# A gated linear attention with a cosine layer: transposes through DRAM, a shorter pipeline, group 0 in chunks, a later weight guard

## The chip, the cores and the metric

The kernel runs on one core of one Trainium2 chip. The time is the device time of one execution in microseconds, as the median of several runs. The names used below are TensorE or PE (matmuls), PEld (weight loads), DVE (VectorE), ACT (ScalarE), POOL (GpSimd) and SP (the engine that issues nearly all transfers, in order).

## The reference

```python
scale = np.minimum(mag, 0.999) / (mag + 1e-06)          # mag = |a|
for t in range(S):                                      # B, H, S, D = 4, 8, 768, 48
    S_re, S_im = a * S (complex) + k[t] v[t]^T
    y[t] = q[t] @ S_re
x = y as (3072, 384)
h = x @ w_in                                            # w_in (384, 2048), double precision
out = (h * cos(h)) @ w_out                              # w_out (2048, 384), double precision
```

The kernel works in chunks of 128 steps, two chunks to a group, twelve groups. For each group it makes *gates* (log, sums by matmul, exponentials, angles, sine and cosine), *squares* (k and q times the gates, transposed to kT and qT), *chunks* (scores, state, output yT), x (yT put into the layout of the layer, xT), the *first layer* (`hp`, with the cosine gate) and the *second layer* (`op`). The weights come in double precision and are converted to single precision by bit operations. A guard looks at their exponents.

## The kernel before

The squares are transposed in 32 x 32 blocks by DVE, and 12 transfers of 32 KB per chunk and tensor put the blocks in place, from SBUF to SBUF:

```python
def f_transpose(n, name):
    tr = ft.tile([C, NR, H, 32], F32, tag="tr", name="tr")
    nc.vector.transpose(out=tr, in_=...)
    ...
    for a in range(Q4):
        for b in range(NR):
            nc.sync.dma_start(out=place[ts(b, 32), a], in_=tr[ts(a, 32), b])
```

x goes the same way, in ten transfers. The order of work is four stages deep; one iteration works on four groups:

```python
for it in range(NG + 3):
    g, c, m, o = it, it - 1, it - 2, it - 3
    ...                                   # g_log, g_prod, g_angle of group g
    for i in range(G): mm2(o, i)          # second layer of group o
    weave((gates(g), 0.0, 0.5), (chunks(c), 0.0, 1.0),
          (weights.get(it, ()), 0.0, 1.0),
          ([mm1(m, jp) for jp in range(NJ // 2)], 0.0, 1.0))   # first layer of group m
```

`weave` sorts the pieces of its parts by their place between the two numbers. The program that builds the kernel (the builder) takes this as a priority and may move a piece ahead. What it decides is then each engine's fixed order.

## Time and profile before

| | before |
|---|---|
| time | 821.7 us (821.4 to 823.4) |
| period of a group in the dense part | 56.9 us, of which PE busy 55.6 |
| first matmul of the second layer | 169 us |
| PE busy in all | 697 us of 823 |

### The profile page before, as it was taken

The page shows a single profiled execution, that of the slowest core. Times are in us where ns is not written, and L with a number is a line of the kernel's source. Part 1 is how long each engine was busy: PE and PEld are TensorE (multiplying, and loading weights), DVE is VectorE, ACT ScalarE, POOL GpSimd, SP SyncE. Part 2 cuts the span into 40 slices and gives each one's busy share as a digit, 9 for nine tenths or more (in the row PEclk, how much of TensorE's full clock was granted, in tenths as well). Part 3 has the DMA queues.
Part 4 walks back from the last instruction along what each step waited for, and adds up shares of the span by engine and source line. Part 5 has one row for each costly group of instructions (what it writes and reads, how often), then busy time and mean ns, then how long its engine had stood idle before and what let it go on. Part 6 is the DMA issues. An engine that isn't in the chain of part 4 may idle for free.

```text
span 823.1 us, 10293 instructions
## 1 busy us (share of the span) xinstructions
PE 697.1 (85%) x3464; PEld 514.9 (63%) x3464; DVE 488.7 (59%) x754; ACT 376.4 (46%) x576; POOL 146.6 (18%) x96
## 2 busy tenths in 40 slices
PE   1217286766899999999999989999999999999997
PEld 0006174534575785876867857858758668677674
DVE  2876454957685574864954856757658458234060
ACT  5552615663666345453571562464545624123140
POOL 1341124322401113003012021040040120000000
PEclk9956576897999999999999999999999999999999
DMA  9624257545632722623625427226236231210000
GB/s 178 128 47 71 45 128 192 129 103 115 164 80 49 150 45 62 119 49 68 112 51 92 84 49 135 42 54 123 49 62 110 51 73 30 49 40 21 20 0 23
DMA packets 251481, 65.67 MB, mean 80 GB/s; under 512 B 230414, under 2 KB 247823, under 8 KB 251419
## 3 DMA queue, kind: packets, MB, share of 16 engines
q1 hardware_dynamic: 250818, 64.62, 38.6%
q8 instruction: 29, 0.48, 0.3%
q10 hardware_dynamic: 600, 0.30, 0.2%
q14 instruction: 34, 0.27, 0.1%
HBM read 36.51 MB, written 4.76 MB: 50 GB/s over the span
## 4 chain that ended last, share of the span: by engine, by line
PE 53%; SPq 15%; DVE 12%; ACT 9%; issue 4%; DMA 3%; POOL 3%; DVEq 0%; ACTq 0%; POOLq 0%
PE hp L823 20%; PE op L841 18%; SPq L753 12%; PE sc L764 3%; ACT rs L629 2%; PE lgs L672 2%; POOL m L656 2%; PE phs L709 2%; PE yp L778 2%; PE sp L795 2%; DVE gate L833 2%; PE phs L712 1%; PE yp L782 1%; ACT L628 1%; SPq L545 1%
## 5 line engine op out<-in xcount | busy, mean ns | idle before, releaser
L823 PE MATMUL hp<-xT,w_in 128*128 128x256 f32 x1152 | 272.9, 390 | 16.0 <-DMA xT<-yT 8.6
L841 PE MATMUL op<-w_out,gate 128*128 128x384 f32 x768 | 256.3, 490 | 17.3 <-POOL w_out L600 17.1
L823 PEld LDWEIGHTS hp<-xT,w_in 128*128 128x128 f32 x1152 | 218.4, 194 | 53.1 <-DVE gate L835 8.7
L841 PEld LDWEIGHTS op<-w_out,gate 128*128 128x128 f32 x768 | 145.8, 191 | 118.5 <-POOL w_out L600 21.3
L829 ACT ACTIVATE turn<-hp,quarter_b 128x512 f32<-128x512 f32 x96 | 65.5, 683 | 91.4 <-PE hp L823 90.2
L629 ACT ACTIVATE gate<-gate 128x512 f32<-128x512 f32 x96 | 60.2, 628 | 102.4 <-DVE gate L833 102.3
L835 DVE TENSOR_TENSOR gate<-hp,gate 128x512 f32<-128x512 f32 x96 | 65.5, 685 | 38.8 <-ACT gate L629 38.4
L831 DVE TENSOR_SCALAR gate<-turn 128x512 f32<-128x512 f32 x96 | 40.7, 427 | 61.9 <-ACT turn L829 61.0
L672 PE MATMUL lgs<-m,sums 128*128 128x384 f32 x48 | 25.1, 657 | 52.2 <-POOL m L656 52.2
L833 DVE TENSOR_TENSOR gate<-turn,gate 128x512 f32<-128x512 f32 x96 | 67.2, 702 | 1.7
L801 POOL TENSOR_TENSOR state<-state,end 96x384 f32<-96x384 f32 x16 | 16.8, 1050 | 266.2 <-DVE state L799 175.2
L844 ACT ACTIVATE ot<-op 128x384 f32<-128x384 f32 x24 | 11.6, 484 | 114.4 <-PE op L841 114.4
L764 PEld LDWEIGHTS sc<-qT,kT 96*128 96x128 f32 x384 | 53.0, 206 | 15.6 <-issue 9.8
L764 PE MATMUL sc<-qT,kT 96*128 96x128 f32 x384 | 53.5, 290 | 7.4 <-issue 4.1
L656 POOL TENSOR_TENSOR m<-m,rs 128x768 f32<-128x768 f32 x12 | 21.7, 1808 | 178.0 <-ACT rs L629 178.0
L672 PEld LDWEIGHTS lgs<-m,sums 128*128 128x128 f32 x48 | 10.6, 245 | 64.7 <-POOL m L656 59.8
L714 DVE TENSOR_SCALAR ph<-phs 128x384 f32<-128x384 f32 x24 | 13.3, 555 | 55.7 <-PE phs L712 40.8
L709 PE MATMUL phs<-sq,sums 128*128 128x384 f32 x48 | 23.0, 570 | 27.2 <-DVE sq L700 27.2
L766 DVE TENSOR_TENSOR atm<-sc,causal 128x512 f32<-128x512 f32 x48 | 32.6, 682 | 18.8 <-PE sc L764 18.6
L659 DVE SCALAR_TENSOR_TENSOR sq<-mag,sq 128x768 f32<-128x768 f32 x12 | 11.5, 958 | 49.1 <-POOL mag L658 49.1
L778 PE MATMUL yp<-atm,v 128*48 128x128 f32 x384 | 38.2, 288 | 0.0
L729 POOL TENSOR_TENSOR Q<-k,Q 128x768 f32<-128x768 f32 x12 | 25.6, 2130 | 55.8 <-ACT rs L697 19.7
(75 smaller groups left out, 812.6 us busy)
## 6 DMA issues: line engine op xcount, KB each, us to landing
kT<-tr SPq DMA_DIRECT2D x288, 32.0 KB, 2.0
qT<-tr SPq DMA_DIRECT2D x288, 32.0 KB, 1.8
raw<-in_moe_w_in_dram SPq DMA_DIRECT2D x12, 512.0 KB, 4.8
raw<-in_moe_w_out_dram SPq DMA_DIRECT2D x16, 384.0 KB, 3.8
re<-in_a_re_dram SPq DMA_DIRECT2D x24, 192.0 KB, 3.0
im<-in_a_im_dram SPq DMA_DIRECT2D x24, 192.0 KB, 4.1
k<-in_k_dram SPq DMA_DIRECT2D x24, 192.0 KB, 4.0
q<-in_q_dram SPq DMA_DIRECT2D x24, 192.0 KB, 4.6
```

The costliest lines, as they stand in the source:

```text
L629: chain(nc.scalar.activation(func=func, **kw))
L672: nc.tensor.matmul(ps, lhsT=sums, rhs=x["lg"][:, ts(i, DM)], start=True, stop=True)
L709: nc.tensor.matmul(ps, lhsT=sums, rhs=x["turn"][:, ts(i, DM)], start=True, stop=first)
L753: nc.sync.dma_start(out=place[ts(b, 32), a], in_=tr[ts(a, 32), b])
L764: nc.tensor.matmul(ps[:, h], lhsT=y["kT"][:, hh * HH + h], rhs=queries(y, hh * HH + h), start=True, stop=True)
L778: nc.tensor.matmul(ps[ds(side * 64, D), p], lhsT=vals[:, 2 * p + side], rhs=y["atm"][:, 2 * p + side], start=True, stop=(state is None))
L823: nc.tensor.matmul(ps[:, ji], lhsT=w_in[:, dc, ts(jp * 2 + ji, C)], rhs=x["xT"][:, dc].rearrange("p g t -> p (g t)"), start=(dc == 0), sto ...
L829: nc.scalar.activation(out=turn, in_=ps, func=AF.Identity, scale=INV_TWO_PI / in_scale, bias=quarter_b)
L831: nc.vector.tensor_scalar(out=cs, in0=turn, scalar1=ROUND, scalar2=ROUND, op0=ALU.add, op1=ALU.subtract)
L833: nc.vector.tensor_tensor(out=cs, in0=turn, in1=cs, op=ALU.subtract)
L835: nc.vector.tensor_tensor(out=gate, in0=ps, in1=cs, op=ALU.mult)
L841: nc.tensor.matmul(ps, lhsT=X[g]["gate"][j // 2][:, j % 2, ts(i, C)], rhs=w_out[:, j], start=(j == 0), stop=(j == NJ - 1))
```

## The change

The intent: SP is relieved of its many small transfers; a group's chunks and its first layer lie in the same iteration, so that the pipeline is one stage shorter; group 0 goes through the gates chunk by chunk with its products on DVE; the guard leaves the start and reads the weights a second time later. The core of the diff (cut: the pass of `i, n` through all gate functions, the split of group 0, temporaries that share buffers):

```diff
-        for a in range(Q4):
-            for b in range(NR):
-                nc.sync.dma_start(out=place[ts(b, 32), a], in_=tr[ts(a, 32), b])
+        moved = rows_d.tile([Q4, D2, n * H, 32], F32, tag="moved", name="moved", bufs=3)
+        nc.sync.dma_start(out=moved.rearrange("q (r b) x j -> (q r) b x j", b=NB), in_=tr)
+        if name == "kT":
+            for q4 in range(Q4):
+                nc.sync.dma_start(out=X[g][name][:, ds(i * H, n * H), q4], in_=moved[q4])
+        else:
+            nc.sync.dma_start(out=X[g][name][:, :, ds(i * H, n * H)],
+                              in_=moved.rearrange("q c x j -> c q x j"))
 ...
     def f_xt(g):
-        (ten transfers yT -> xT)
+        moved = rows_d.tile([HH, 2, D, G * C], F32, tag="x", name="x")
+        for side in range(2):
+            nc.sync.dma_start(out=moved[:, side]..., in_=X[g]["yT"]...)
+        nc.sync.dma_start(out=xt..., in_=moved...)
 ...
-    weights = {1: parts[:-NJ], 2: parts[-NJ:]}
-    for it in range(NG + 3): ...
+    conversions = {(-1, 1): into, (0, 0): back[:NJ // 2], (0, 1): back[NJ // 2:]}
+    for c in range(-1, NG + 1):
+        ...
+        weave((gates_a(c + 1), 0.0, 0.3),
+              (chunks(c) if c >= 0 else (), 0.0, 0.9),
+              (extra(c, 0), 0.0, 1.0),
+              (second(c - 1), 0.0, 1.0))
+        weave((gates_b(c + 1), 0.0, 0.5),
+              (extra(c, 1), 0.0, 1.0),
+              (first(c) if c >= 0 else (), 0.0, 1.0))
```

An iteration now has two halves. The first holds the gates up to the phase sums of the next group, the chunks of this one and the second layer of the last one. The second half holds the rest of the gates and this group's first layer. `extra` is conversion of weights at first and guard later.

## The prediction

> **What bounds the kernel now.** I read the page's forty slices first, then busy time in three stretches, then the chain of work that ended last, and last the timeline of the sync engine (SP) in the first 80 us. Rows of the slices:
>
> ```profile
> PE   1217286766899999999999989999999999999997
> PEclk9956576897999999999999999999999999999999
> DMA  9624257545632722623625427226236231210000
> ```
>
> Each digit is 20.6 us. The matrix engine (PE) is a tenth or two busy in the first three slices, around 70% until the tenth, and at 90% or more in nearly every slice after that. So there are two regimes, and the border is near 258 us, where the gate sums of the fifth group start. Busy time on both sides of it (columns: stretch, its length, then busy time and instruction count of PE, weight loads, DVE, ACT, POOL, the granted clock, the DMA share, GB/s):
>
> ```profile
> 0.00:257.80 257.80, 149.24 (x678) 106.75 (x678) 164.25 (x263) 134.08 (x216) 70.56 (x54) 0.80 0.52 112
> 257.80:713.00 455.20, 444.54 (x2320) 332.92 (x2321) 292.77 (x438) 216.21 (x318) 74.87 (x42) 1.00 0.39 75
> 713.00:823.00 110.00, 103.32 (x467) 75.18 (x465) 31.64 (x53) 26.10 (x42) 1.21 (x1) 0.99 0.08 23
> ```
>
> The middle stretch is eight groups: 56.9 us each, of which PE works 444.54 / 8 = 55.6 us. It is bound by PE at 98%. Twelve groups of 55.6 us are 667 us of PE work at full clock. From 257.8 us on PE does 444.5 + 103.3 = 548 us of it, so before 257.8 us it did 119 us' worth, at a mean clock of 0.80. The start therefore loses 258 - 119 = 139 us; the rest loses 565 - 548 = 17 us, 6 of them in the check of the flags at the end. 667 + 139 + 17 = 823. Whatever the change gains has to come out of the 139.
>
> What fills the start: the chain of waits names SP's queue, and SP's timeline shows why.
>
> ```profile
> PE 53%; SPq 15%; DVE 12%; ACT 9%; issue 4%; DMA 3%; POOL 3%; DVEq 0%; ACTq 0%; POOLq 0%
> ```
>
> ```profile
> 41.84 7.98 SPq L753 DMA_DIRECT2D kT<-tr  x12
> 49.92 7.53 SPq L753 DMA_DIRECT2D qT<-tr  x12
> 57.55 7.85 SPq L753 DMA_DIRECT2D kT<-tr  x12
> 65.50 7.86 SPq L753 DMA_DIRECT2D qT<-tr  x12
> 73.40 3.03 SPq L685 DMA_DIRECT2D end<-row  x6
> ```
>
> Twelve transfers of 32 KB take 7.8 us to issue, 0.65 us each, back to back for 31.6 us. During this the DMA engines are only 23 to 32% busy (windows 40 to 80 us). Scores of chunk 0 wait for the 24th issue (PE starts them at 64.8), those of chunk 1 for the 48th (75), and the weights wait behind. Even in the steady part SP issues for 48 x 0.65 + 10 x 0.63 (x) + 6 x 0.48 (end) + some 8 (loads, out) = 48 of 57 us.
>
> ```profile
> kT<-tr SPq DMA_DIRECT2D x288, 32.0 KB, 2.0
> raw<-in_moe_w_in_dram SPq DMA_DIRECT2D x12, 512.0 KB, 4.8
> raw<-in_moe_w_out_dram SPq DMA_DIRECT2D x16, 384.0 KB, 3.8
> out_dram<-ot SPq DMA_DIRECT2D x24, 192.0 KB, 3.2
> xT<-yT SPq DMA_DIRECT2D x72, 48.0 KB, 2.0
> ```
>
> The last column is the time from issue to landing; it sizes the new transfers below.
>
> **What the Trainium skill says.** "Perfetto Trace Analysis", section What "DMA-bound" means, counts a solid issuing track as a bound of its own, apart from the movement of data; the trace agrees (SP solid for 31.6 us, engines a third busy). "DMA: Bandwidth & Descriptors", Rules for kernel authors, wants many small transfers joined, since under 64 KB one pays mostly overhead, and a transfer that reads what another wrote must wait for its semaphore. The first agrees: 32 KB cost 0.65 us of queue and 192 KB loads about the same. The second is the price of going through DRAM. "TensorE: Matmul & The Clock Gate", What's actually happening, has a half-rate state after idle windows; here the clock is 0.50 from 40 to 60 us and 1.00 when dense. "SBUF — State Buffer", section SBUF: two separate sides, says that DVE and GpSimd lock each other out; the same weight operation on DVE takes 0.42 us alone and 2.03 us beside GpSimd's product at 23.2 us.
>
> **The change part by part.**
> Squares: per group 48 issues become 2 writes, 4 reads of kT and 1 of qT; x 10 become 3; end 6 become 2. 64 issues become 12. At 0.5 to 1 us each SP saves about 40 - 9 = 31 us per group. In the steady part this is worth nothing directly, as PE is the bound there. In the start it is on the path.
> Bytes: each square now moves twice, in packets of 2 KB except kT's read, which still scatters 128 B. Per group DMA work falls out as: loads 10 x 1.05 us (192 KB at the 184 GB/s of the first 20 us at full share), kT read 6144 packets of 128 B at about 22 ns over 16 engines, 8.5 us (an estimate from what is left of 0.42 x 57 us of a steady group), other square traffic 2.4 MB at some 300 GB/s, 8 us. About 27 us per group in all.
> Group 0 per chunk: operations of 0.96 us become two of 0.55, products go from POOL (1.8 to 2.2 us) to DVE. First results come out some 4 us sooner. Scores of chunk 0: phase sums now at 30.6 us come near 22, stacked by 27, then write 3.5, kT read 3.5, qT write and read 6: near 42 instead of 64.8.
> Guard later: 28 DVE operations (17.4 us) and 28 ACT ones (18.4 us) leave the start; 12.6 MB are read again in groups 3 to 9, two tiles per half iteration, where DMA has room (0.4 busy).
> One stage fewer: the first layer matmul of group 0 follows its chunks in the same iteration. It starts at 128 us now. New: chunks end near 58 us, x is there near 68. Gates of 20.7 us of first-layer work end near 95 if DVE keeps up: DVE has in this iteration 20 (gates of group 1) + 15 (w_out, 16 x 0.94) + 4 (scores) + 14.6 (8 x 1.82) = 54 us after some 45 in the iteration before, so about 100. DMA until then: 2.5 groups of loads 26, weights 12.6 MB at 300 GB/s 42, two groups of squares 33, x 3: 104 us of 16 full engines. DMA and DVE both say PE gets dense at 105 to 115 us; I take 112, with 45 us' worth of PE work done (gates of two groups 9, chunks 10 to 15, first layer 21). Loss in the start 67 instead of 139: gain 72.
> The cost: before, x had a whole iteration to arrive. Now it lies between chunks and first layer of one group: copies to yT 1.2, one more issue 0.5, write as out<-ot 3.2, read as a 384 KB weight tile 3.8, semaphores 0.3: 9 us, each group. After the second chunk's output PE still has two pieces of the second layer (2 x 8 matmuls x 0.323 = 5.2 us) and often part of the 3.2 us of phase sums. Exposed: 1 to 4 us, plus delay by other traffic. I take 3 us x 11 = 33, which includes the 1.3 us of gaps that a group has now.
> Sum: 667 + 67 + 33 + 6 = 773.
>
> **Rivals.**
> (a) x hidden after all: the builder already moves work a long way (second-layer matmuls run ahead of gate sums emitted before them; the squares of the next group start 25 us early). If it fills the gap, 1.3 us per group: about 755.
> (b) x, or kT and qT, late: SP waits in order, so a wait for a DRAM write holds the read behind it; guard tiles of 512 KB sit in front of x. The square chain is now write, wait, read, write, wait, read, some 18 us where it used to be 31 of issue. At 7 us per group: 815, all the gain nearly gone. For it: a period of 57 has to hold gates, squares, chunks, x and first layer over two iterations, about 103 of 114 us by my count, which is little slack. Against: SP is freed by 31 us.
> (c) DMA bandwidth or DVE holds the start longer, PE dense only at 130: 790.
> (d) Second half of an iteration bound by DVE (14.6 + 8 = 22.6 us against 20.7 of PE): 2 us per group, 795 with the rest; unlikely to add fully, since the stack can be moved ahead.
>
> **Range and chances.** Most likely between the sum and a little of (b): 775. Eight in ten: 745 (a shorter start, x hidden) to 812 (b, or c and d together). Faster by over 2% means under 805: 0.84. Within 2%: 0.11. Slower: 0.05; that would need over 9 us lost in each group.
>
> **What would show it.** PE's slices at 90% from the sixth on; first hp matmul near 70 us and first op near 100; SP for the squares down from 576 issues to about 90; PE's total near 690. Idle of hp put down to DMA xT: 20 to 40 us shows the price of x; 70 or more shows (b), near 5 shows (a). PE idle put down to qT or kT would show the squares late. I am wrong if PE's dense part has a period over 61 us per group, or if it starts after 130.

## More of the kernel before

The prediction shows the slices, the windows and SP's queue. One more view: the order of PE inside one iteration of the dense part. These are lines of PE's timeline (start, length, engine and line, operation, names, shapes, count, and the idle time before it with what ended it):

```profile
314.67 1.56 PE L672 MATMUL lgs<-m,sums 128*128 128x384 f32 x4 [1.69 <-POOL m L656]
316.07 12.42 PE L841 MATMUL op<-w_out,gate 128*128 128x384 f32 x38
328.32 0.81 PE L709 MATMUL phs<-sq,sums 128*128 128x384 f32 x2
...
334.39 1.06 PE L764 MATMUL sc<-qT,kT 96*128 96x128 f32 x8
335.28 2.76 PE L823 MATMUL hp<-xT,w_in 128*128 128x256 f32 x12
337.87 1.48 PE L795 MATMUL sp<-v,ks 128*96 128x48 f32 x16
339.19 2.82 PE L823 MATMUL hp<-xT,w_in 128*128 128x256 f32 x12
```

Between the log sums (lgs) and the phase sums (phs), whose inputs ACT and DVE have to make, PE does 12.4 us of second layer. Between the steps of a chunk (sc, sp) it does first layer of another group. The only wait in the iteration is the 1.69 us at lgs. (In these views the trace has two records for each matmul of the code: 96 hp for the 48 of a group, 64 op for 32.)

## The result, and the profile after

The changed kernel takes 849.4 us (844.7 to 853.9, 4 runs) against 821.7. The ratio is 1.033, with a 95% interval of 1.027 to 1.039: it is slower, clear of noise. A ratio is the mean time of one kernel's runs over that of the other's of the same rounds, so it is not quite the ratio of the medians that are quoted. The profiled execution is the fastest of the four, with a span of 842.9 us. The four runs spread over 9 us and differ in their mean granted clock, the share of full speed that PE was given: 0.959 and 0.957 in the two faster ones, 0.940 and 0.932 in the two slower. So the profile shows somewhat less loss than the median has. Its slices:

```profile
PE   1236298799889989989989989989989989989996
PEclk9999599999989999999999999999989999999999
DMA  9877796896680680580670671670770670170100
```

Each digit is now 21.1 us. The start is better than before: PE is at 70% or more from the sixth slice on, where before it stood at 60 to 80% from the sixth to the eleventh. But from there on the row repeats "989", with a dip in every third slice, once in each group, and this goes on to the end. Before, the row was nines. The same in one stretch of both dense parts, first before, then after (columns as in the prediction):

```profile
386.90:699.50 312.60, 304.73 (x1625) 231.11 (x1625) 206.75 (x313) 151.55 (x222) 49.36 (x28) 0.99 0.39 74
```

```profile
386.90:699.50 312.60, 282.65 (x1421) 208.25 (x1420) 192.98 (x262) 143.18 (x204) 53.45 (x26) 0.97 0.48 102
```

PE was busy 97.5% of this stretch and is now busy 90%, and in the same 312.6 us it gets through 1421 matmuls instead of 1625. No other engine took its place: DVE is 62% busy, ACT 46%. Six periods, taken from one lgs to the sixth after it, are 63.1 us each (331.99 to 710.81), against 56.9 before (314.67 to 655.91). Eleven periods at 6.2 us more make 68 us. That is where the time went. What PE waits for in the dense part of the changed kernel, from 192 to 815 us (total us, times, longest):

```profile
PE hp L850 <- DMA xT<-x: 29.8, 10, 4.1
PE phs L727 <- DVE tan L719: 14.8, 9, 3.6
PE lgs L692 <- POOL lg L675: 11.7, 9, 1.3
```

And PE's order in one iteration, which answers to the one shown of before:

```profile
426.43 22.41 PE L850 MATMUL hp<-xT,w_in 128*128 128x256 f32 x96 [4.01 <-DMA xT<-x]
448.68 1.06 PE L790 MATMUL sc<-qT,kT 96*128 96x128 f32 x8
449.57 7.91 PE L870 MATMUL op<-w_out,gate 128*128 128x384 f32 x24
458.77 1.56 PE L692 MATMUL lgs<-lg,sums 128*128 128x384 f32 x4 [1.29 <-POOL lg L675]
460.17 1.06 PE L790 MATMUL sc<-qT,kT 96*128 96x128 f32 x8
461.06 6.62 PE L870 MATMUL op<-w_out,gate 128*128 128x384 f32 x20
469.07 0.91 PE L727 MATMUL phs<-tan,sums 128*128 128x384 f32 x2 [1.40 <-DVE tan L719]
...
480.80 5.43 PE L870 MATMUL op<-w_out,gate 128*128 128x384 f32 x16
488.61 1.35 PE L850 MATMUL hp<-xT,w_in 128*128 128x256 f32 x5 [2.38 <-DMA xT<-x]
```

All 96 matmuls of the first layer now stand in one block behind x. Ahead of them are the last 16 of the second layer, 5.4 us. PE stands still three times in a group: at lgs, at phs (20 matmuls lie between the two instead of 38) and at hp. There is a fourth loss that no wait shows. The 96 hp matmuls take 22.4 us here. They take 20.99 us in the groups where the pause before them left the clock alone (group at 741.72 below). In the eleven groups from 169 us on, the excess over 20.99 adds up to 15.7 us; in the six periods measured above it is 1.6 us a group. In one such block the granted clock is 0.50 from 300.4 to 302.4 us and 1.00 before the pause and from 303.4 on. The way of x in one group, from the chain of work that ended last (start, length, what):

```profile
734.46 0.59 ACT yT L812
735.06 3.04 DMA x<-yT
738.11 0.02 SPq L841
738.13 0.03 issue
738.16 3.52 DMA xT<-x
741.68 0.04 issue
741.72 20.99 PE hp L850 x96
```

Store 3.0, load 3.5, with the copies 7.9 us from the last output (733.8) to the first hp.

In the start x of group 0 has a trouble of its own. SP's timeline:

```profile
80.45 0.38 SPq L837 DMA_DIRECT2D x<-yT  x1
87.45 3.44 SPq L590 DMA_DIRECT2D raw<-in_moe_w_out_dram  x3
90.94 0.42 SPq L837 DMA_DIRECT2D x<-yT  x1
92.18 2.27 SPq L590 DMA_DIRECT2D raw<-in_moe_w_out_dram  x2
95.26 0.38 SPq L841 DMA_DIRECT2D xT<-x  x1
```

The outputs are complete at 77 us. The second store of x goes out 10.5 us after the first, because loads of w_out stand between the two and SP, taking its list in order, waits for their buffers. hp starts at 100 after 23.3 us of idle PE.

### The profile page after: what moved, and what is told of

The parts are those of the page before. It is cut to its first block, busy times and chain, and to the rows that moved or that the text cites. A ratio compares the mean times of both kernels' runs of the same rounds, so it can differ in the third digit from the quotient of the medians. Undisturbed runs are those within 1.5% of the kernel's fastest.

```text
span 842.9 us, 9481 instructions
## 1 busy us (share of the span) xinstructions
PE 700.1 (83%) x3464; PEld 514.9 (61%) x3464; DVE 528.2 (63%) x757; ACT 382.6 (45%) x589; POOL 154.7 (18%) x92
## 5 line engine op out<-in xcount | busy, mean ns | idle before, releaser
L850 PE MATMUL hp<-xT,w_in 128*128 128x256 f32 x1152 | 270.1, 399 | 56.2 <-DMA xT<-x 56.2
L850 PEld LDWEIGHTS hp<-xT,w_in 128*128 128x128 f32 x1152 | 230.7, 201 | 97.7 <-DMA xT<-x 63.2
L870 PEld LDWEIGHTS op<-w_out,gate 128*128 128x128 f32 x768 | 142.3, 190 | 91.9 <-issue 2.2
L675 POOL TENSOR_TENSOR lg<-lg,rs 128x768 f32<-128x768 f32 x11 | 20.0, 1814 | 374.8 <-ACT rs L637 374.2
L812 ACT COPY yT<-yp 48x512 f32<-48x512 f32 x48 | 27.7, 578 | 54.2 <-PE yp L808 41.0
L727 PE MATMUL phs<-tan,sums 128*128 128x384 f32 x48 | 24.8, 607 | 31.8 <-DVE tan L719 29.3
L768 DVE STREAM_TRANSPOSE tr<-qs 128x1536 f32<-128x1536 f32 (+1 forms) x13 | 26.7, 2052 | 36.3 <-DMA moved<-tr 36.3
L692 PE MATMUL lgs<-lg,sums 128*128 128x384 f32 x48 | 23.2, 609 | 28.0 <-POOL lg L675 15.7
L827 POOL TENSOR_TENSOR state<-state,end 96x384 f32<-96x384 f32 x16 | 26.6, 1663 | 103.3 <-DVE state L825 60.1
L792 DVE TENSOR_TENSOR atm<-sc,causal 128x512 f32<-128x512 f32 x48 | 32.8, 684 | 10.5 <-PE sc L790 10.5
L821 PEld LDWEIGHTS sp<-v,ks 128*96 128x96 f32 x320 | 31.9, 174 | 3.9 <-issue 2.4
L677 DVE SCALAR_TENSOR_TENSOR tan<-mag,tan 128x768 f32<-128x768 f32 (+1 forms) x13 | 11.6, 895 | 35.9 <-POOL mag L676 35.8
```

The lines of the kernel that those rows point to most:

```text
L792: nc.vector.tensor_tensor(out=y["atm"][:, ts(hh, HH)], in0=ps, in1=causal.unsqueeze(1).to_broadcast([C, HH, C]), op=ALU.mult)
L812: nc.scalar.copy(out=X[g]["yT"][half, :, i], in_=ps[half])
L821: nc.tensor.matmul(ps[:, h], lhsT=keys, rhs=X[g]["v"][:, i, h], start=True, stop=True)
L850: nc.tensor.matmul(ps[:, ji], lhsT=w_in[:, dc, ts(jp * 2 + ji, C)], rhs=x["xT"][:, dc].rearrange("p g t -> p (g t)"), start=(dc == 0), sto ...
L870: nc.tensor.matmul(ps, lhsT=X[g]["gate"][j // 2][:, j % 2, ts(i, C)], rhs=w_out[:, j], start=(j == 0), stop=(j == NJ - 1))
```

## The experiments

Three theories were set against each other. A: the order of work leaves PE nothing to do while x travels, and the pause also costs clock. B: the doubled traffic (102 MB against 66) slows the groups. C: DVE holds them. All kernels gave correct results. "Period" is again over six groups, from one whose lgs lies between 270 and 335 us. The runs below were made in four sets, each with its own runs of the kernel before (medians 821.6 to 823.6), so differences of a few us between runs of different sets are not clear.

| run | what | time us | ratio to before | period us |
|---|---|---|---|---|
| before | | 821.7 | 1 | 56.9 |
| changed | | 849.4 | 1.033 | 63.1 |
| e1_chunks_early | new order, chunks in 0.55 of the half | 812.2 | 0.988 | 59.4 |
| e2_x_direct | new order, x in ten transfers | 829.4 | 1.011 | 62.0 |
| e3_warm | new order, useless matmuls in the pause | 834.5 | 1.015 | 62.1 |
| e4_first_later | new order, layers one iteration later | 818.4 | 0.999 | 58.2 |
| e5_wout_after_x | new order, w_out later | 842.1 | 1.026 | 62.6 |
| e6_squares_direct | new order, squares as before | 882.8 | 1.074 | 64.8 |
| e9_guard_inline | new order, guard as before | 846.8 | 1.030 | 63.2 |
| e10_first_and_weights_later | e4 and weights later | 806.1 | 0.980 | 58.4 |
| b1_combo | e1, e3, e5 together (0.45, 3 matmuls) | 817.5 | 0.992 | 59.2 |
| e8_before_squares | before, squares through DRAM | 794.6 | 0.965 | 56.2 |
| b2_old_order | changed, old order | 785.6 | 0.954 | 56.4 |
| b3_old_order_w0 | b2, weights early | 802.8 | 0.975 | 56.4 |
| b4_old_order_inline | b3, guard as before | 796.0 | 0.968 | 56.1 |
| b5_old_order_guard_inline | b2, guard as before | 790.1 | 0.961 | 56.1 |
| b6_old_order_group0_whole | b2, group 0 whole | 799.7 | 0.973 | 56.2 |
| b7_old_order_x_direct | b2, x in ten transfers | 782.5 | 0.952 | 56.4 |

**Chunks earlier in the half.**

```diff
-              (chunks(c) if c >= 0 else (), 0.0, 0.9),
+              (chunks(c) if c >= 0 else (), 0.0, 0.55),
```

> Only the place of a group's chunks in the first half of an iteration changes: they are spread over its first 0.55 instead of 0.9. Theory A (x travels while PE has too little second-layer work left, and the pause then costs a slow restart of the clock): pieces of the second layer left after the last chunk's output go from 2 (16 matmuls, 5.4 us) to 4 (10.3 us), more than the 7.7 us that x takes. The waits of hp for xT after 190 us fall from 29.8 us to under 6, hp takes 21.0 us in every group instead of 22.7, the period falls from 62.8 to about 58, and the time from 849 to about 795. Theory B (the doubled DMA traffic of squares through DRAM, 121 GB/s against 80, is what slows the groups): no wait disappears, time within 1% of 849. Theory C (DVE, 528 us busy against 489, holds the groups): same as B.

812.2 us, 37 less than the changed kernel. B and C fall as the main cause: bytes and DVE's work are the same. A's size was missed, since not 54 us but 37 were gained. PE and SP in one group (lines left out between):

```profile
464.77 8.01 PE L870 MATMUL op<-w_out,gate 128*128 128x384 f32 x24
...
465.49 0.94 SPq L837 DMA_DIRECT2D x<-yT  x2
466.47 0.78 SPq L545 DMA_DIRECT2D v<-in_v_dram  x1
...
470.14 0.38 SPq L841 DMA_DIRECT2D xT<-x  x1
...
474.87 1.35 PE L850 MATMUL hp<-xT,w_in 128*128 128x256 f32 x5 [2.10 <-DMA xT<-x]
```

The fill grew only to 8.0 us, as some of the second layer still went ahead. x itself took 10 us instead of 7.9, now that its store meets the loads of the next group. A pause of 2 us is left: from 192 to 815 us the waits for x are 19.2 us (29.8 before the edit), not under 6. The gain has two other parts. The waits at phs fall from 14.8 to 2.3 us, and five of the six hp blocks from 357 to 652 us take 20.99 us, so the slow clock is nearly gone too.

**x by the old route.** The three transfers of `f_xt` are replaced by the ten of the kernel before:

```diff
-        moved = rows_d.tile([HH, 2, D, G * C], F32, tag="x", name="x")
-        (two stores yT -> moved, one load moved -> xt)
+        for h in range(H):
+            row = h * D
+            while row < (h + 1) * D:
+                n = min((h + 1) * D, (row // C + 1) * C) - row
+                nc.sync.dma_start(out=xt[ds(row % C, n), row // C],
+                                  in_=X[g]["yT"][ds(h % 2 * 64 + row - h * D, n), h // 2])
+                row += n
```

> x goes from SBUF to SBUF in ten transfers again, all else as changed. Theory A: the ten issues of 0.6 us and 2 us to landing take about as long (8 us) as the trip through DRAM (7.7), so waits of hp stay near 30 us and the time within 1.5% of 849: the place of the transfer matters, not its route. Theory B (DRAM trips are slow): the waits fall below 15 us and the time to 820 or less.

829.4 us, 20 less: more than A allowed for, less than B asked. Group 0's hp starts at 93 instead of 100, and in the dense part the period is 62.0. In the dense part (192 to 815 us) the waits for x fall from 29.8 to 9.5 us, which B expected and A did not, but 14.9 us of waits at hp for DVE's gates take their place. The trip through DRAM costs something where x is urgent; most of the 6 us by which the period had grown are not its route.

**Useless matmuls in the pause.**

```diff
+        if 0 <= c < NG:
+            warm()          # 4 matmuls 128x384 of w_in into a spare PSUM tile, not read
         weave((gates_b(c + 1), 0.0, 0.5),
```

> Four useless matmuls pairs of 128x384 (some 2.6 us) fill PE between the last second-layer matmul and the first layer of each group; their result is not read. Theory A, clock part: the pause of PE shrinks to 1.5 us or less, hp takes 21.0 us instead of 22.7 in nearly all groups, and 8 to 11 x 1.7 = 13 to 18 us are gained: about 833. If the clock is no part of it (the longer hp is something else, such as waits for DVE): time within 0.5% of 849 or slower by up to 1%.

834.5 us, as expected: 15 us gained by doing more (8 between the two profiled runs). The group shown above of the changed kernel, with the pause filled:

```profile
421.83 2.74 PE L928 MATMUL warm<-w_in,sums 128*128 128x384 f32 x8
426.17 20.99 PE L850 MATMUL hp<-xT,w_in 128*128 128x256 f32 x96 [1.59 <-DMA xT<-x]
```

Every hp block from 172 us on takes 20.99 us or less. So the longer hp was the clock and nothing that DVE or a buffer did. The period falls by 1.1 us and not by the 1.6 of the clock: the useless matmuls and the wait that is left take about 3.5 us a group, where the wait alone took 3.0.

**Layers one iteration later.**

```diff
-              (second(c - 1), 0.0, 1.0))
+              (second(c - 2), 0.0, 1.0))
 ...
-              (first(c) if c >= 0 else (), 0.0, 1.0))
+              (first(c - 1) if c >= 1 else (), 0.0, 1.0))
```

> The first and second layer of a group come one iteration later than its chunks, as in the kernel before; all else as changed (squares and x through DRAM, group 0 per chunk, guard later). Theory A: waits of hp for xT after the start vanish (under 5 us), period 57 to 58; the start is longer by the stage that was saved: PE dense at 165 to 185 instead of 124. Sum about 667 + 125 + 20 + 7 = 820. Theory B or C: period stays at 61 or more, and the time is 870 or more.

818.4 us, as A expected. From 330 to 620 us its PE waits are only these:

```profile
PE lgs L692 <- POOL lg L675: 7.4, 5, 1.6
PE phs L727 <- DVE tan L719: 7.0, 5, 1.4
```

The wait for x and the slow clock after it are gone, and the period falls by 4.9 us to 58.2, close to what the two cost in the changed kernel (3.0 + 1.6 a group). The waits at lgs and phs stay. The start is worse: PE waits 26.6 us for x of group 0 (the fifth slice is at 0), and the first op starts at 168 instead of 124.

**w_out after x.**

```diff
-    conversions = {(-1, 1): into, (0, 0): back[:NJ // 2], (0, 1): back[NJ // 2:]}
+    conversions = {(-1, 1): into, (0, 1): back}
```

> All sixteen w_out tiles are converted in the second half of group 0's iteration instead of eight in each half, so that no w_out load stands before x of group 0 on SP. In the changed kernel PE waits 23.3 us for this x, and its second store is issued at 90.9 us though the outputs are there at 77. If SP's order is the cause: first hp near 86 instead of 100, and 8 to 14 us less in all, about 838. If DMA bandwidth or the conversions are the bound of the start: the second layer waits for w_out in its place and the time stays within 0.5% of 849.

842.1 us. hp starts at 85.8 us, as expected, and the first op at 112 instead of 124, so SP's order was what held x of group 0. Only 7 of the 14 us are left at the end: the second group's hp starts at 162 against 169. A gain in the start is handed on only in part.

**Guard on the loaded tile, in the new order.** The three guard operations go back behind the conversion, and the second read is left out:

```diff
-    def guard(src):
-        n = src.shape[-1]
-        raw = stage.tile([C, n], I64, tag="raw", name="raw", bufs=3)
-        nc.sync.dma_start(out=raw, in_=src)
-        hi = raw.bitcast(U32).rearrange("p (x two) -> p x two", two=2)[:, :, 1]
 (the three operations on hi follow, now inside weight())
...
-    guards = [src for _, src in into + back if src.dtype != F32]
+    guards = []
```

> The guard works on the tile that was loaded for the conversion again (no second read of 12.6 MB); all else as changed. In the changed kernel the second reads ran from 128 to 245 us, and the periods there are 69 and 66 us against 63 later. If that traffic costs: these two fall to 63 or so, 9 us less, while the start gets longer by at most 10 (28 x 0.6 us more on DVE and ACT): 840 to 850. If the guard's move was a real gain in the start: over 855.

846.8 us, no difference that counts. Both expected effects are there and cancel: the two periods of 68.0 and 65.6 us fall to 63.9 and 62.4, and the two before them grow by 5.6 together. The trace of the changed kernel shows that the guard was not moved far at all: SP issues second reads from 128.7 to 245 us, with one stretch of twelve in a row.

```profile
186.34 20.07 SPq L606 DMA_DIRECT2D raw<-in_moe_w_out_dram  x12
```

The builder brought the work ahead. Its inputs need nothing but a free buffer, which would explain it; no run tests this.

**The squares alone, in the kernel before.** `f_transpose`, the layout of ks and qs and the end row of the changed kernel; to make room, 10 gate buffers for 11 and two shared temporaries. Order, x, group 0 and guard as before. Beside the functions taken over:

```diff
-        e = stage.tile([C, n], U32, tag="e", name="e", bufs=1)
+        e = stage.tile([C, n], U32, tag="low", name="e")
...
-        x["P"], x["Q"] = temp("P"), temp("Q")
+        x["P"], x["Q"] = x["lg"], temp("Q")
...
-        gate = msb.tile([C, 2, G * C], F32, tag="gate", name="gate", bufs=11)
+        gate = msb.tile([C, 2, G * C], F32, tag="gate", name="gate", bufs=10)
```

> The kernel before with the squares and the end row through few transfers and DRAM, and nothing else but what memory asks for (10 gate buffers, two shared temporaries); order, x and guard as before. If SP's issue time bounds the start, as predicted: 48 issues a group go, the start loses 20 to 35 us less, the dense part keeps its period of 57: 787 to 800. If the doubled traffic costs more than the issue time gave (theory B): 820 or more, with waits for qT or kT on PE.

794.6 us, 27 less than before, in the expected range. The first op starts at 154 instead of 169, and the period is 56.2 against 56.9, so most of the gain lies in the start. So the part that the prediction put first is right, and DRAM traffic as such (theory B) does no harm.

**All three patches together in the new order.** Chunks in 0.45, w_out after x, three useless matmuls:

```diff
-              (chunks(c) if c >= 0 else (), 0.0, 0.9),
+              (chunks(c) if c >= 0 else (), 0.0, 0.45),
...
-    conversions = {(-1, 1): into, (0, 0): back[:NJ // 2], (0, 1): back[NJ // 2:]}
+    conversions = {(-1, 1): into, (0, 1): back}
...
+        if 0 <= c < NG:
+            warm()          # 3 matmuls
```

> Chunks in the first 0.45 of the half, w_out after x, and three pairs of useless matmuls before the first layer. By theory A the steady period falls to 58 and x of group 0 no longer waits behind w_out: 849 - 37 (chunks early, measured) - 8 (w_out) - 5 (clock) = about 798, less than both kernels.

817.5 us: a miss, 19 us over the expectation and no better than e1 alone. The gains do not add. In e1 most hp blocks were at full clock already, so the useless matmuls had little left to save. The waits for x shrink to 19.2 us in all (e1: 40.7), but those for phs are 20.6 (e1: 14.2), and in one late group the builder left 12 matmuls between lgs and phs, so PE waited 4 us there and fell to the slow clock. Here, patching the place of one piece moved the pause to another.

**All of the change except its order.** The loop of the kernel before around the functions of the changed one; group 0 stays in chunks and the guard comes from iteration 4:

```diff
-    for c in range(-1, NG + 1):
-        (two weaves, as shown under "The change")
+    conversions = {1: into, 2: back}
+    for it in range(NG + 3):
+        g, c, m, o = it, it - 1, it - 2, it - 3
+        (g_log, g_prod, g_angle of group g by its spans)
+        if 0 <= o < NG:
+            for i in range(G):
+                mm2(o, i, 0, NJ)
+        weave((gates(g) if g < NG else (), 0.0, 0.5),
+              (chunks_v(c) if 0 <= c < NG else (), 0.0, 1.0),
+              (extra(it), 0.0, 1.0),
+              (first(m) if 0 <= m < NG else (), 0.0, 1.0))
```

> All parts of the change (squares and x through DRAM, group 0 per chunk, guard later) except the order: gates, chunks, first layer and second layer of four different groups in one iteration, first-layer pieces spread among the chunks, as in the kernel before; w_in and w_out in iterations 1 and 2 as before. If the order alone is the loss: period 56 to 57, waits of hp for xT in the dense part under 3 us, and 780 to 797. If x through DRAM or the second read of the weights costs as well: over 805.

785.6 us, 64 less than the changed kernel and 36 less than before, in the expected range. The stretch that was shown of the other two, and the order around lgs:

```profile
386.90:699.50 312.60, 304.53 (x1597) 228.67 (x1596) 196.50 (x276) 138.34 (x205) 47.57 (x27) 0.99 0.45 97
```

```profile
272.05 1.56 PE L692 MATMUL lgs<-lg,sums 128*128 128x384 f32 x4 [1.11 <-POOL lg L675]
273.44 12.42 PE L870 MATMUL op<-w_out,gate 128*128 128x384 f32 x38
285.69 0.81 PE L727 MATMUL phs<-tan,sums 128*128 128x384 f32 x2
```

At 97 GB/s, nearly the 102 of the changed kernel, PE is busy 97% again. The 38 matmuls between lgs and phs are back, and so is the first layer between the steps of the chunks. This settles B and C.

**Weights early, in the old order.** Against b2:

```diff
-    conversions = {1: into, 2: back}
+    conversions = {0: into, 1: back}
```

> As b2_old_order, with w_in converted in iteration 0 and w_out in iteration 1 (the changed kernel's place). If the conversions hold the start: hp starts before 100 us, and 5 to 15 us less than b2_old_order. If they get in the way of group 0's gates: the same or more.

802.8 us: 17 more, and hp starts at 134 instead of 106. The log sums of the second and third group come 6 and 18 us later, so the early conversions do get in the way of the gates; on which engine was not looked at.

**The same with the guard on the loaded tile.** b3 with the diff of e9, whose core is:

```diff
-    guards = [src for _, src in into + back if src.dtype != F32]
+    guards = []
```

> As b3_old_order_w0, with the guard on the tile already loaded. If the second read is a gain: 3 to 12 us more than b3_old_order_w0 (28 more operations of 0.6 us on DVE and on ACT in the start). If it is only traffic: the same or less.

796.0 us, 7 less than b3: in this crowded start the second read was a loss.

**Old squares in the new order.** The reverse of e8's functions, in the changed kernel:

```diff
-        (one store to moved, then four loads for kT or one for qT)
+        for a in range(Q4):
+            for b in range(NR):
+                nc.sync.dma_start(out=place[ts(b, 32), a], in_=tr[ts(a, 32), b])
```

> The changed kernel with the squares from SBUF to SBUF in 48 transfers a group and the end row in six, as before; the new order kept. If squares through DRAM are a gain in either order: the start is 20 to 35 us longer and the issues also delay x (SP in order), 870 or more. If the new order gets along as well with the old squares (theory B, traffic): 849 or less.

882.8 us, 33 more than the changed kernel. The squares through DRAM are worth about the same in either order (27 and 33).

What was still open was the other half of the 64 us, and the worth of the small parts.

**Layers and weights one iteration later, in two halves.** The diff of e4, and:

```diff
-    conversions = {(-1, 1): into, (0, 0): back[:NJ // 2], (0, 1): back[NJ // 2:]}
+    conversions = {(0, 0): into[:6], (0, 1): into[6:], (1, 0): back[:NJ // 2], (1, 1): back[NJ // 2:]}
```

> The changed kernel's two halves with both layers one iteration later (as in e4_first_later, 818) and in addition the weights one iteration later, as in b2_old_order. If the early weights hold the start by standing before x and group 1's gates on SP and DVE: the wait of 26.6 us for x of group 0 goes, and 800 or less. If the rest is due to the two halves themselves (second layer and first layer apart, gate sums waiting 1.5 to 3 us a group): 812 to 825.

806.1 us, between the two expectations: 12 less than e4, and the wait for x of group 0 falls from 26.6 to 9.7. Early weights are 12 us of it. The 20 us that are left to b2 lie with the two halves: the period is 58.4 against 56.4, 2 us a group, which are the phs waits (1.4) and a little more. So the 64 us between the changed kernel and b2 are about 31 for the layers in the same iteration as the chunks (e4), 12 for the early weights and 20 for the two halves.

**Guard on the loaded tile (diff of e9), group 0 whole (below), and x direct (diff of e2), each in b2.**

```diff
     def spans(g):
-        return [(i, 1) for i in range(G)] if g == 0 else [(0, G)]
+        return [(0, G)]
...
-        mult = nc.vector if g == 0 else nc.gpsimd
+        mult = nc.gpsimd
```

> b2_old_order (786) with the guard on the loaded tile. With the weights early this gained 7 us. If the second read only costs traffic: 776 to 784. If the guard's work is better out of the start: 788 to 795.

> b2_old_order (786) with group 0 in one piece and its products on GpSimd, as in the kernel before. The first gate sums come at 10 us per chunk instead of 16 for both: if that stage sets the start, 5 to 10 us more, 791 to 796; if the weights set it, no change within 3 us.

> b2_old_order (786) with x from SBUF to SBUF in ten transfers. In the old order x has an iteration to arrive, so its route should not matter: within 4 us of 786. If the ten issues of 0.6 us still held SP in the start: 3 to 8 us more.

790.1: with the weights late, the guard's second read is a gain of 4.5 us by the medians, the opposite sign of b3 and b4; b5 and b2 ran in different sets and the intervals of their ratios touch, so it is not clear of noise. 799.7: group 0 in chunks is worth 14 us, more than expected. 782.5: with an iteration to spare, the route of x does not matter (3 us less when direct). The last is the fastest kernel, 0.952 of before, though it and b2 are close and ran in different sets.

## Why the prediction was wrong

It said 775 us, in a range of 745 to 812, and gave a slower kernel a chance of 0.05. By its own steps:

- **What bounds the kernel: right.** The dense part is PE's and its work did not change (700 us busy against 697). The old-order variants keep 56.1 to 56.4 us.
- **Squares: right.** SP's 31 us of issue per group were on the path of the start and hardly on one later (period 0.7 us less in e8). e8 measured 27 us, e6 33.
- **Group 0 per chunk: right in sign, too small.** It was put at 4 us plus what follows; b6 measured 14.
- **Guard later: wrong in its working.** "Groups 3 to 9" did not happen; the second reads fell between 128 and 245 us. Its worth changed sign with the rest: the second read cost 3 us in the changed kernel (within noise) and 7 in b3, and gained 4.5 in b2.
- **The shorter stage: mis-sized.** The start was to lose 67 us, with PE dense at 112 us and 45 us' worth of work done. PE got dense at 124, with 40 done, a loss of 84. The 12 us are x of group 0 waiting behind w_out on SP (e5: hp at 85.8 once they are out of the way). Of the steps inside, the chunks of group 0 ended at 77 us and not at 58 (PE waited 9.2 us for the phase sums of group 1 between them), and x took 23 us and not 10. The prediction's sum for the start counted DVE and DMA, and not the order of SP.
- **The cost of x: the step that failed.** "I take 3 us x 11 = 33, which includes the 1.3 us of gaps that a group has now." Measured were 63.1 - 55.6 = 7.5 us, 83 in eleven. The wait for x alone was 3.0, inside the stated 1 to 4, but the sum left only 1.7 for it. The term held too little for three further things: the slow clock after the pause (1.6, shown by e3), the waits at phs that came in when second and first layer were put into separate halves (about 1.5; b2 has none from 330 to 620 us), and the gaps of before (1.3 at lgs), which stayed beside it. The skill's clock gate stood in the prediction, and was used for the start only.
- **The rivals.** (b) had the right size, "at 7 us per group: 815" (its own terms give 817), but not the cause. It came with the wrong start, 17 us too short, and it blamed SP: reads held behind a DRAM write, guard tiles in front of x. In the group shown of the dense part SP began to issue the load of x within 0.02 us of the store's landing (the chain above), and without guard tiles (e9) the period stayed at 63.2 us and the waits for x at 30.5. SP's order held x in group 0 only. That the size came out was luck. Against (b) stood that "SP is freed by 31 us": SP was free, and x was late all the same. (a) rested on the builder filling the gap. In the order that it built, nothing stands between the last op and hp.
- **Its own signs.** A period over 61 us was to prove it wrong, and it was 63.1. The idle time of hp put down to x was 56.2 us in all, between the signs for the stated price (20 to 40) and for (b) (70 or more); 23.3 of it were at group 0. One slip of reading changed nothing: the fifth slice of the kernel before is at 20%, not around 70%.

667 + 84 + 83 + 7 (the end) = 841, against a span of 842.9 of the profiled run. The 40 us done before 124 are an estimate from the matmuls that had run by then.

## What to carry to other kernels

A pipeline stage that lies between a transfer and its use is not only latency in the start; it is what the bound engine works on while the transfer travels. Before taking it out, list in order what that engine has left to do from the issue to the landing, and count the clock it loses if the list is too short. Test the parts of a change one by one: here squares through DRAM (-27 us) and the new order with its early weights (+64 us) came in one change and hid each other.

## What the Trainium skill lacked or had wrong

- "TensorE: Matmul & The Clock Gate", What's actually happening: the slow state is said to come after at least one idle window of about 3.4 us. Here pauses of 2.4 us before hp were followed by the slow clock in some groups (22.67 us for the block at 299.39 and 678.21 us) and not in others (20.99 us at 488.61). Of the eleven groups from 169 us on, the six with pauses of 3.1 to 4.1 us were all slowed, two of the four with 2.4 to 2.6 us, and not the one with 1.7. The free-running window that the page describes may account for the scatter; as a threshold, 3.4 us is too generous.
- The same page, its rule that such gaps are to be avoided: filling the pause with useless matmuls gained 15 us of 849 (e3); the page doesn't name this remedy.
- "DMA: Bandwidth & Descriptors", Rules for kernel authors: joining transfers held (48 issues a group became 7, 27 us gained), but no section has the cost of a pair of dependent transfers through DRAM issued from SP; the page's fit of time to size is for transfers that GpSimd issues. For 384 KB it was 3.0 us for the store and 3.5 for the load, and 10 us in all beside other loads.
- The same section's measure by bytes says nothing on how the time to issue depends on the shape: stores of 768 KB took SP 0.33 to 1.4 us, reads of 192 KB with 128-byte pieces 1.0 us in the median, and 32 KB from SBUF to SBUF 0.6 us.
- "Perfetto Trace Analysis", What "DMA-bound" means: it has the solid issuing track, but not the other way in which SP delays work: a transfer that is ready, behind one that waits for a buffer (10.5 us between the two stores of x at 80 and 91 us, with SP far from solid).
